# A transformer block on one core: values computed per 64-key block into the attention layout, two chunks with the in-engine softmax division, another order

## The chip, the core and the metric

The kernel runs on one core of a Trainium2 chip. The metric is device microseconds of one execution. The engines of the core work side by side, each through its own list of instructions in order: PE multiplies matrices (its weight loads are listed as PEld), DVE and ACT do element work and empty the accumulators (`ps`, 8 banks), POOL does small element work, SP (and at the start ACT) issues the transfers, which share 16 DMA engines.

## What is computed

One sequence of 2048 tokens, width 448, in bf16. Cut to what matters:

```python
def _A_ref(x, wqkv, wo):                 # x = layernorm(input)
    q, k, v = split(x @ wqkv)            # 16 heads of 28
    # token s looks at the 8 keys s, s-2, ..., s-14 of its own parity (masked below 0)
    attn = softmax(q . k[idx] * 28**-0.5)
    return (attn @ v[idx]) @ wo
def _B_ref(x, w1, w2, w3, w4):           # x = layernorm(h)
    g = gelu(layernorm(x) @ w1)          # 448 wide
    hs = shift4(g) @ w2                  # quarters shifted by -1, +1, -2, +2 tokens
    x1 = x + hs
    return x1 + gelu(layernorm(x1) @ w3) @ w4    # 1792 wide
h   = x + _A_ref(layernorm(x), wqkv, wo)
out = h + _B_ref(layernorm(h), w1, w2, w3, w4)
```

## The kernel before

The tokens are cut into four chunks of 512 (`c` = 0 to 3), each kept as two runs of 256 tokens of even and of odd parity, so that a query sees 8 neighbouring keys of its run. For attention, a run's keys are taken in `NB` = 5 overlapping blocks of 64 (`KS` = 50 apart), the queries in blocks of 51 or 52. Everything is written as operations with declared reads and writes; the list `_ORDER` (line 232) fixes the order on every engine and the bank of each accumulator, and waits follow from the declared reads and writes. The numbers that the helpers take as costs are not used when the kernel runs.

Per chunk these steps run, each line being the code that the prediction's names refer to:

- **A1** (`phase_A1`, 536): layernorm of the tile (BN_STATS, BN_AGGR on DVE; 1/sqrt on POOL; the scaling into `lntm` on DVE or ACT), then the transposition into `hT`. Chunks 0 and 1 (`TPE`) transpose on PE, 16 small matmuls a chunk, and copy to `hT`; chunks 2 and 3 with one DMA transposition of four tiles, issued by SP.
- **V** (`phase_V`, 558): v = hT x wv, 28 matmuls of 64 rows, 128 columns and 448 streamed columns, each pair on the upper and the lower half of the array (`quad`, 368). The result is copied to `vraw`, written by two transfers to a scratch array in DRAM and read back by two more as `vt`, the five 64-key blocks of each parity, key on the partition.
- **QK** (`phase_QK`, 576): q and k, 56 matmuls, into `qk`.
- **S**, **AV** (`phase_att`, 592): 80 small matmuls for the scores of half the heads (`g` = 0, 1), exp on ACT into `pt`, a mask multiplication on DVE, 80 small matmuls with `vt`. One column of `vt` is a constant, so that the sum of each row comes along.
- **Division by that sum**: chunk 0 (`FAST`) with `norm_blocks` (642): for each of its four blocks a 32x32 transposition out of the bank, a reciprocal, a multiplication and a transposition back, all on DVE. Chunks 1 to 3 with `norm_dma` (656): a copy to `osb`, transfers that gather the sums, a reciprocal, a transfer to DRAM, four transfers that spread it, four multiplications on DVE.
- **WO** (`phase_WO`, 680), **B1** (`phase_B1`, 693: residual, two layernorms, W1 and gelu into `gT`), **B2** (W2 and a layernorm), **W3** (`phase_W3`, 750: a transposition by DMA, the adds tagged `R`, W3 and gelu), **B3** (W4, residual, output). B2, W3 and B3 run over five groups of tiles, `g` = 0 to 4, two or four tiles each.

In the program's order S, AV and their neighbours of chunk 0 to 2 stand between the QK and V of later chunks; W1 of chunk 0 comes after S of chunk 2; from WO of chunk 3 on, PE has only W1 to W4 left. SP issues every load of weights, every transposition by DMA and every scratch transfer in one list.

## Time and profile before

| | |
|---|---|
| median of 3 runs | 216.14 us (215.55 to 216.34) |
| the profiled execution | 216.01 us |
| its span, first to last instruction | 214.2 us |
| PE busy | 183.7 us (86%) |
| DVE busy | 120.5 us (56%) |
| ACT, POOL busy | 92.1 us, 52.5 us |
| bytes moved by DMA | 23.53 MB |

The span is the time from the first to the last instruction of the profiled execution; its own time is 1.8 us longer. Busy shares are averages over the whole span. "Issue" as a releaser means that the engine stood idle and waited for nothing that the profile shows. A merged row of the timeline stands for a run of equal matmuls: start, length, and in brackets the idle time ahead of it and what ended it.

### The profile page before, as it was taken

The numbers are of one execution on the slowest core, as the hardware profiler recorded it, in microseconds if no ns is written. First come the engines' busy times: TensorE is split into PE (matmuls) and PEld (weight loads), VectorE is DVE, ScalarE is ACT, GpSimd is POOL, SyncE is SP. The second block draws the span as 40 slices with busy tenths as digits, with TensorE's granted clock in tenths as the row PEclk, the third lists the DMA queues.
The fourth block names the chain that finished last, engine by engine and source line by source line (L and its number), as shares of the span: only waits on it lengthen the run. The fifth ranks groups of instructions, "written<-read, shape, count | busy, mean of one in ns | idle before, by whom it ended". The sixth has DMA issues, their size and how long they took to land.

```text
span 214.2 us, 6051 instructions
## 1 busy us (share of the span) xinstructions
PE 183.7 (86%) x2687; PEld 99.9 (47%) x2687; DVE 120.5 (56%) x250; ACT 92.1 (43%) x111; POOL 52.5 (24%) x108
## 2 busy tenths in 40 slices
...
PEclk9759999999799999999999999999999999999998
DMA  5995949799199924940051870035400091000111
GB/s 149 356 267 138 261 78 252 169 163 268 30 130 200 315 47 81 234 122 0 3 101 54 107 180 18 24 59 123 81 0 0 21 171 43 0 3 6 43 46 49
DMA packets 37568, 23.53 MB, mean 110 GB/s; under 512 B 22800, under 2 KB 36768, under 8 KB 37536
## 3 DMA queue, kind: packets, MB, share of 16 engines
...
## 4 chain that ended last, share of the span: by engine, by line
PE 48%; DVE 18%; DMA 16%; issue 6%; ACT 4%; POOL 4%; SPq 2%; ACTq 0%
PE ps L1236 48%; DMA actT<-lntm 7%; DVE st L1236 5%; DVE xb L1236 5%; DMA rzb<-rz_scratch 4%; DMA arena<-in_A_wqkv_dram 3%; DVE lntm L1236 2%; DVE xin L1236 2%; ACT qk L1236 2%; SPq L1236 2%; DMA rz_scratch<-rzp 2%; POOL rstd L1236 1%; POOL xb L1236 1%; DVE oT L1236 1%; DVE mv L1236 1%
## 5 line engine op out<-in xcount | busy, mean ns | idle before, releaser
L1236 PE MATMUL ps<-actT,w_s 64*128 64x512 bf16 (+3 forms) x672 | 56.1, 323 | 6.7 <-DMA actT<-lntm 3.6
L1236 PEld LDWEIGHTS ps<-actT,w_s 64*128 64x128 bf16 (+1 forms) x672 | 34.5, 99 | 27.8 <-ACT arena L1236 3.3
L1236 PE MATMUL ps<-w_s,arena 128*128 128x448 bf16 x224 | 43.5, 353 | 0.0
L1236 DVE TENSOR_TENSOR xb<-ps,xb 128x448 bf16<-128x448 f32 (+1 forms) x24 | 18.3, 771 | 32.7 <-PE ps L1236 32.7
L1236 ACT ACTIVATE arena<-ps 128x512 bf16<-128x512 f32 (+2 forms) x40 | 28.4, 766 | 17.3 <-PE ps L1236 17.3
L1236 PEld LDWEIGHTS ps<-w_s,arena 128*128 128x128 bf16 x224 | 21.7, 98 | 20.4 <-issue 0.4
L1236 PE MATMUL ps<-hT,arena 64*128 64x512 bf16 x224 | 28.0, 403 | 1.1 <-DVE hT L1236 0.5
L1236 POOL TENSOR_SCALAR vtmp<-mv 128x4 f32<-128x4 f32 (+1 forms) x18 | 4.7, 259 | 91.0 <-DVE mv L1236 90.1
L1236 DVE BATCH_NORM_STATS2 st<-xin 128x6 f32<-128x448 bf16 x32 | 18.4, 608 | 1.1 <-DMA xin<-in_A_x_dram 0.9
L1236 PEld LDWEIGHTS ps<-hT,arena 64*128 64x128 bf16 x224 | 10.9, 100 | 16.0 <-issue 3.4
L1236 ACT ACTIVATE pt<-ps 128x1024 bf16<-128x1024 f32 x16 | 15.5, 1023 | 6.5 <-PE ps L1236 6.5
L1236 ACT ACTIVATE qk<-ps 128x1024 bf16<-128x1024 f32 x10 | 10.1, 1024 | 17.7 <-PE ps L1236 17.7
L1236 POOL TENSOR_TENSOR rstd<-vtmp,mhalf 128x4 f32<-128x4 f32 (+1 forms) x18 | 17.3, 962 | 1.0
L1236 POOL TENSOR_TENSOR xb<-xb,xin 128x448 bf16<-128x448 bf16 x16 | 16.8, 1067 | 2.7 <-ACT lntm L1236 1.9
L1236 PE MATMUL ps<-wo_s,oT 128*128 128x448 bf16 x64 | 13.8, 353 | 3.8 <-issue 2.4
L1236 DVE SCALAR_TENSOR_TENSOR oT<-osb,rzb 128x512 bf16<-128x512 f32 x12 | 7.5, 686 | 14.8 <-DMA rzb<-rz_scratch 14.8
L1236 ACT ACTIVATE lntm<-xb,nmr,rstd 128x512 bf16<-128x512 bf16 x7 | 5.5, 810 | 21.6 <-POOL nmr L1236 21.6
L1236 DVE TENSOR_TENSOR pt<-pt,msk 128x1024 bf16<-128x1024 bf16 x16 | 11.7, 738 | 3.1 <-ACT pt L1236 3.1
L1236 DVE SCALAR_TENSOR_TENSOR xin<-ps,xin 128x896 bf16<-128x896 f32 x8 | 8.6, 1073 | 8.2 <-PE ps L1236 8.2
L1236 PE MATMUL ps<-w_s,gT 112*128 112x448 bf16 x64 | 13.1, 353 | 0.0
L1236 PE MATMUL ps<-arena,hT 64*128 64x448 bf16 x112 | 11.4, 350 | 0.4 <-ACT qk L1236 0.4
L1236 PE MATMUL ps<-pt,vt 64*32 64x51 bf16 (+1 forms) x640 | 6.9, 190 | 5.5 <-issue 4.2
...
## 6 DMA issues: line engine op xcount, KB each, us to landing
rzb<-rz_scratch SPq DMA_DIRECT2D x12, 256.0 KB, 4.3
...
vt<-v_scratch SPq DMA_DIRECT2D x8, 320.0 KB, 5.8
v_scratch<-vraw SPq DMA_DIRECT2D x8, 256.0 KB, 3.7
...
```

The source lines that it names most:

```text
L1236: inst = getattr(eng, meth)(**kw)
```

## The change

**Values.** `hT` gets 8 more columns per parity ahead of a chunk's 256 (copied from the chunk before by POOL), and a layout in which 64 neighbouring keys of one parity are contiguous. V now takes a 64-key block of each parity as its weights and writes the result to the partitions where attention wants it: per chunk 56 matmuls of 64 rows, 64 columns and 448 streamed columns in `quad`, in groups of four that use the four quarters of the array, and 8 of 128 rows and 64 columns for the fifth block (with `wv_2`, a copy of one weight window whose upper half is zero). The banks are copied straight to `vt`, three copies where there were two (896, 896 and 448 elements a partition). `vraw`, the scratch array, its two zero writes, eight writes and eight reads are gone.

**Division.** `FAST` is now chunks 0 and 1: chunk 1 uses `norm_blocks`.

**Moved.** The 16 adds tagged `R` and the zeroing of `wo_s` go from POOL to DVE. The DMA transposition of chunks 2 and 3 is issued tile by tile (eight instead of two). The V weights are loaded ahead of the others.

**Order.** All of `_ORDER` is new. Three places:

PE from its start: the warm-up matmuls (oT), the transpositions of chunk 0 (ident), QK (hT,arena), V (arena,hT; wv_2), the scores S (qk). Before:

```order
L1236 MATMUL ps<-oT 128x512 x14
L1236 MATMUL ps<-ident,lntm 128x128 x16
L1236 MATMUL ps<-hT,arena 128x512 x28
L1236 MATMUL ps<-arena,hT 128x448 x28
L1236 MATMUL ps<-qk 64x52 x8
L1236 MATMUL ps<-qk 64x51 x32
L1236 MATMUL ps<-qk 64x52 x8
L1236 MATMUL ps<-qk 64x51 x32
```

and now:

```order
L1256 MATMUL ps<-oT 128x512 x14
L1256 MATMUL ps<-ident,lntm 128x128 x16
L1256 MATMUL ps<-arena,hT 64x448 x4
L1256 MATMUL ps<-wv_2,hT 64x448 x2
L1256 MATMUL ps<-arena,hT 64x448 x46
L1256 MATMUL ps<-hT,arena 128x512 x28
L1256 MATMUL ps<-arena,hT 64x448 x12
L1256 MATMUL ps<-ident,lntm 128x128 x16
```

V of chunk 0 now stands ahead of the first QK, the last 12 of its matmuls behind it, and 64 matmuls stand where 28 did.

PE ahead of the first W1 (actT,w1_s), where before the second half of QK of chunk 2 (x56), S of chunk 2, V of chunk 3 and S again stand:

```order
L1236 MATMUL ps<-hT,arena 128x512 x56
L1236 MATMUL ps<-qk 64x52 x8
L1236 MATMUL ps<-qk 64x51 x32
L1236 MATMUL ps<-qk 64x52 x8
L1236 MATMUL ps<-qk 64x51 x32
L1236 MATMUL ps<-arena,hT 128x448 x28
L1236 MATMUL ps<-qk 64x52 x8
L1236 MATMUL ps<-qk 64x51 x32
L1236 MATMUL ps<-qk 64x52 x8
L1236 MATMUL ps<-qk 64x51 x32
L1236 MATMUL ps<-actT,w1_s 112x512 x28
```

and now the end of AV of chunk 1 (pt,vt), the first 8 matmuls of V of chunk 3, and the second half of S of chunk 2:

```order
L1256 MATMUL ps<-pt,vt 32x52 x8
L1256 MATMUL ps<-pt,vt 32x51 x32
L1256 MATMUL ps<-pt,vt 32x52 x8
L1256 MATMUL ps<-pt,vt 32x51 x32
L1256 MATMUL ps<-arena,hT 64x448 x4
L1256 MATMUL ps<-wv_2,hT 64x448 x2
L1256 MATMUL ps<-arena,hT 64x448 x2
L1256 MATMUL ps<-qk 64x52 x8
L1256 MATMUL ps<-qk 64x51 x32
L1256 MATMUL ps<-qk 64x52 x8
L1256 MATMUL ps<-qk 64x51 x32
L1256 MATMUL ps<-actT,w1_s 112x512 x28
```

V of chunk 3 is mostly behind W1 now, and AV, V and S of three chunks stand close together.

DVE around the division of chunk 1. Before, it has the reciprocal of the gathered sums (rzp<-zp) and, later, four multiplications (oT<-osb,rzb); in between stand copies, scalings (lntm, xb) and masks (pt):

```order
L1236 CAST qk<-ps 128x4x256
L1236 RECIPROCAL rzp<-zp 128x64
L1236 TENSOR_SCALAR lntm<-xin,mv,rstd 128x512 x3
L1236 CAST qk<-ps 128x4x256
L1236 TENSOR_SCALAR xb<-xin,mv,rstd 128x448 x2
L1236 TENSOR_TENSOR pt<-pt,msk 128x1024
L1236 CAST vraw<-ps 128x32x28
L1236 TENSOR_TENSOR pt<-pt,msk 128x1024 x3
L1236 SCALAR_TENSOR_TENSOR oT<-osb,rzb 128x2x256 x4
L1236 COPY osb<-ps 128x1024
```

and now the division of its first half, with scalings for chunk 0 between its steps:

```order
L1256 STREAM_TRANSPOSE osb<-ps 128x512
L1256 TENSOR_SCALAR lntm<-xin,mv,rstd 128x512 x2
L1256 STREAM_TRANSPOSE osb<-ps 128x512
L1256 TENSOR_SCALAR xb<-xin,mv,rstd 128x448
L1256 RECIPROCAL zp<-osb 128x16
L1256 TENSOR_SCALAR xb<-xin,mv,rstd 128x448
L1256 SCALAR_TENSOR_TENSOR rzb<-osb,zp 128x512
L1256 RECIPROCAL zp<-osb 128x16
L1256 TENSOR_SCALAR xb<-xin,mv,rstd 128x448
L1256 STREAM_TRANSPOSE oT<-rzb 128x2x256
L1256 SCALAR_TENSOR_TENSOR rzb<-osb,zp 128x512
L1256 STREAM_TRANSPOSE oT<-rzb 128x2x256
```

Each block takes a transposition, a reciprocal, a multiplication and a transposition back, and the second half of chunk 1 follows with the same eight instructions.

The diff, cut to its core (of the table the first line stands for all):

```diff
-4 0 18 3 14 17 19 2 1 15 61 20:7 60 76 68 8 12 62 16 69 6 7 63 72 9 70 5 64 11 71 29 93 65 27 13 66 23 28 75 30
+4 0 16 3 56 77 12 15 76 8 1 13 62 17:7 14 61 59 2 9 42 75 60 71 6 7 63 5 69 10 70 73 103 66 26 104 64 24 72 27
...
-    TPE, FAST = (0, 1), (0,)
+    TPE, FAST = (0, 1), (0, 1)
...
-    hT = sb("hT", [128, 2, 4, 4, 128], BF16)
+    hT = sb("hT", [128, 2, 4, 2, 272], BF16)
     qk = sb("qk", [128, 2, 4, 2, 2, 264], BF16)
-    vraw = sb("vraw", [128, 4, 16, 32], BF16)
     vt = sb("vt", [128, 2, NB, 16, 32], BF16)
...
+    wv_2 = sb("wv_2", [128, D], BF16)
...
-    VROW = HALF + 8
-    v_d = nc.dram_tensor("v_scratch", (2 * VROW, 512), BF16, kind="Internal")
...
+        if not isinstance(outs[0], list):
+            outs = [[o] for o in outs]
+            lhsTs = [lambda r, w, f=f: [f(r, w)] for f in lhsTs]
         lo, hi = slice(0, 64), slice(64, 128)
 
         def phase(a, b, ba, bb, first, T):
             mms = []
             for x, y in zip(ba, bb):
-                mms.append((outs[a], lhsTs[a](lo, x), rhss[a](lo, x), first and x == ba[0], not first and x == ba[-1]))
-                mms.append((outs[b], lhsTs[b](hi, y), rhss[b](hi, y), first and y == bb[0], not first and y == bb[-1]))
-            op = pe(mms, len(mms) * (n / 4.8 + 1.5), "half")
+                for k, r, v, bv in ((a, lo, x, ba), (b, hi, y, bb)):
+                    for o, l in zip(outs[k], lhsTs[k](r, v)):
+                        mms.append((o, l, rhss[k](r, v), first and v == bv[0], not first and v == bv[-1]))
+            op = pe(mms, 2 * len(ba) * (n / 4.8 + 1.5), "half")
...
+    win_load("wqk", wqk_s, A_wqkv[:, 0:2 * D], 512 * 2 * D * 2, ("sp", "act"))
     win_load("wv", wv_s, A_wqkv[:, 2 * D:3 * D], 512 * D * 2, ("sp", "act"))
-    win_load("wqk", wqk_s, A_wqkv[:, 0:2 * D], 512 * 2 * D * 2, ("sp", "act"))
...
-    tag("vz")
-    for p in range(2):
-        dma("vz%d" % p, v_d.ap()[p * VROW:p * VROW + 8, :], zz[0:8, :], 8192)
...
-    pool("memset", 312, ap=vraw[:, :, :, 29:32], constant=0.0)
-    pool("memset", 141, ap=vraw[:, :, :, 28], constant=2.0 ** -4)
+    pool("memset", 100, ap=hT[:, 0, :, :, 8:16], constant=0.0)
...
+        for s in range(2):
+            pool("memset", 330, ap=vt[:, s, :, :, 29:32], constant=0.0)
+            pool("memset", 200, ap=vt[:, s, :, :, 28], constant=2.0 ** -4)
...
-        pool("memset", 1589, ap=wo_s[:], constant=0.0)
+        dve("memset", 600, ap=wo_s[:], constant=0.0)
...
-    def transpose_pe(ls, il, dst):
+    def columns(s, il):
+
+        o = 16 + 128 * (il % 2)
+        return hT[:, s, :, il // 2, o:o + 128]
+
+    def transpose_pe(ls, il, s):
...
-        copy(dst[:, il, :, :], T(bv), 512, mode=2.0)
-
-    def transpose_dma(ls, dst, n):
-
-        S.add_many("sp", [("dma_start_transpose", dict(
-            out=dst[:, 0:n, :, :].rearrange("p i w n -> p (i w) n"),
-            in_=lntm[:, ls, 0:n, :, :].rearrange("p i a k -> p (i a k)")))], 600 + 310 * n, 600 + 310 * n,
-            chan="tr%d" % ls, nbytes=n * 131072, fix=600)
+        copy(columns(s, il), T(bv), 512, mode=2.0)
+
+    def transpose_dma(name, dst, src, n):
+
+        S.add_many("sp", [("dma_start_transpose", dict(out=dst, in_=src))], 600 + 310 * n, 600 + 310 * n,
+            chan="tr%s" % name, nbytes=n * 131072, bw=194.0, fix=400)
+
+    def transpose_tiles(ls, dst, n):
+        transpose_dma("%d" % ls, dst[:, 0:n, :, :].rearrange("p i w n -> p (i w) n"),
+                      lntm[:, ls, 0:n, :, :].rearrange("p i a k -> p (i a k)"), n)
...
         for il in range(4):
             normalize(0, 0, 4 * c + il, lntm[:, ls, il, :, :], windows(xin[:, 4 * c + il, :]), dve_only=c == 0)
             if c in TPE:
-                transpose_pe(ls, il, hT[:, s, :, :, :])
-        if c not in TPE:
-            transpose_dma(ls, hT[:, s, :, :, :], 4)
+                transpose_pe(ls, il, s)
+            else:
+                transpose_dma("%d_%d" % (c, il), columns(s, il), lntm[:, ls, il, :, :].rearrange("p a k -> p (a k)"), 1)
+        if c > 0:
+            tag("Vc_%d" % c)
+            pool("tensor_copy", 215, out=hT[:, s, :, :, 8:16], in_=hT[:, 1 - s, :, :, 264:272])
...
     def pad_wqk():
+        tag("padv")
+        dve("memset", 230, ap=wv_2[:], constant=0.0)
+        copy(wv_2[64:128, :], wv_s[64:128, 2, :], D, psum=False, mode=3.0)
...
     def phase_V(c):
+
         s = c % 2
         tag("V_%d" % c)
-        T1, T2 = tile(2), tile(2)
-        quad([T(lambda p, u=u: p[:, u, 0:D]) for T in (T1, T2) for u in range(2)],
-             [lambda r, w, k=k: hT[r, s, k, w, :] for k in range(4)],
+        T1, T2, T3 = tile(2), tile(2), tile()
+        halves = lambda T, u: [T(lambda x, u=u, p=p: x[64 * p:64 * p + 64, u, 0:D]) for p in range(2)]
+        keys = lambda r, w, b: [hT[r, s, w, p, 8 + KS * b:72 + KS * b] for p in range(2)]
+        quad([halves(T, u) for T in (T1, T2) for u in range(2)], [lambda r, w, b=b: keys(r, w, b) for b in range(4)],
              [lambda r, w: wv_s[r, w, :]] * 4, D, T1, T2)
+        tag("V_%d.4" % c)
+        pe([(o, l, wv_2[:] if w == 2 else wv_s[:, w, :], w == 0, w == 3) for w in range(4)
+            for o, l in zip(halves(T3, 0), keys(slice(0, 128), w, 4))], 4 * (D / 2.4 + 2.5), "full")
+        v = lambda p: p[:, :, 0:D].rearrange("p u (j d) -> p u j d", d=28)
         for k, T in enumerate((T1, T2)):
             tag("V_%d.e%d" % (c, k))
-            copy(vraw[:, 2 * k:2 * k + 2, :, 0:28],
-                 T(lambda p: p[:, :, 0:D].rearrange("p u (j d) -> p u j d", d=28)), 2 * D)
-        tag("Vd_%d" % c)
-        for p in range(2):
-            dma("vw%d" % p, bass.AP(v_d, (p * VROW + 8 + 256 * c) * 512, [[512, 128], [128 * 512, 2], [1, 512]]),
-                vraw[:, 2 * p:2 * p + 2, :, :].rearrange("k u j d -> k u (j d)"), 128 * 2 * 1024)
-            dma("vr%d%d" % (s, p), vt[64 * p:64 * p + 64, s, :, :, :].rearrange("k b j d -> k b (j d)"),
-                bass.AP(v_d, (p * VROW + 256 * c) * 512, [[512, 64], [KS * 512, NB], [1, 512]]), 64 * NB * 1024)
+            copy(vt[:, s, 2 * k:2 * k + 2, :, 0:28], T(v), 2 * D)
+        tag("V_%d.e2" % c)
+        copy(vt[:, s, 4:5, :, 0:28], T3(v), D)
...
-                 [lambda r, w: hT[r, s, :, w, :]] * 4, 512, T1, T2)
+                 [lambda r, w: hT[r, s, w, :, 16:272]] * 4, 512, T1, T2)
...
-        transpose_dma(ls, actT[:, a, :, :, :], 4)
+        transpose_tiles(ls, actT[:, a, :, :, :], 4)
...
         for c, il in grp:
             i = 4 * c + il
-            pool("tensor_tensor", 1040, out=xb[:, i, :], in0=xb[:, i, :], in1=xin[:, i, :], op=ALU.add)
+            dve("tensor_tensor", 390, out=xb[:, i, :], in0=xb[:, i, :], in1=xin[:, i, :], op=ALU.add)
```

## Rows read from the trace of the kernel before

**Rows 1.** The page's part 1: busy us, share of the span, instructions.

```profile
PE 183.7 (86%) x2687; PEld 99.9 (47%) x2687; DVE 120.5 (56%) x250; ACT 92.1 (43%) x111; POOL 52.5 (24%) x108
```

**Rows 2.** The page's part 2, 40 slices: granted clock and DMA share in tenths.

```profile
PEclk9759999999799999999999999999999999999998
DMA  5995949799199924940051870035400091000111
```

**Rows 3.** Timeline of PE: start, length, run [idle before <-releaser]; first transpositions, QK, V.

```profile
10.73 2.10 PE L1236 MATMUL ps<-ident,lntm 128*128 128x128 bf16 x16 [4.56 <-DVE lntm L1236]
13.35 4.00 PE L1236 MATMUL ps<-hT,arena 64*128 64x512 bf16 x28 [0.52 <-DVE hT L1236]
17.19 2.81 PE L1236 MATMUL ps<-arena,hT 64*128 64x448 bf16 x28
```

**Rows 4.** Timeline of DVE at the start: the copy of the padded weights, the first scalings.

```profile
8.29 0.40 DVE L1236 COPY arena<-arena 128x896 bf16<-128x896 bf16 x1 [1.69 <-DMA arena<-in_A_wqkv_dram]
8.60 2.72 DVE L1236 TENSOR_SCALAR lntm<-xin,mv,rstd 128x512 bf16<-128x512 bf16 x4
```

**Rows 5.** Timeline of PE: the stops inside runs of matmuls; QK at two speeds.

```profile
35.86 0.55 PE L1236 MATMUL ps<-qk 28*64 28x51 bf16 x47 [0.80 <-issue]
...
39.59 0.23 PE L1236 MATMUL ps<-pt,vt 64*32 64x51 bf16 x11 [1.13 <-issue]
...
47.27 1.88 PE L1236 MATMUL ps<-wo_s,oT 128*128 128x448 bf16 x9 [2.35 <-issue]
...
52.02 0.49 PE L1236 MATMUL ps<-pt,vt 64*32 64x51 bf16 x42 [1.63 <-issue]
52.44 7.90 PE L1236 MATMUL ps<-hT,arena 64*128 64x512 bf16 x56
...
73.26 0.94 PE L1236 MATMUL ps<-pt,vt 64*32 64x51 bf16 x93 [1.45 <-issue]
...
78.78 3.19 PE L1236 MATMUL ps<-hT,arena 64*128 64x512 bf16 x28
```

**Rows 6.** Timeline of PE: 80 matmuls of AV, and the run behind them.

```profile
112.34 0.80 PE L1236 MATMUL ps<-pt,vt 64*32 64x52 bf16 x80 [0.87 <-DVE pt L1236]
113.08 4.72 PE L1236 MATMUL ps<-actT,w_s 64*128 64x256 bf16 x56
```

**Rows 7.** Timeline of PE: the waits ahead of W1, W3 and WO.

```profile
67.83 3.23 PE L1236 MATMUL ps<-actT,w_s 64*112 64x512 bf16 x28 [2.44 <-ACT pt L1236]
...
87.00 5.61 PE L1236 MATMUL ps<-actT,w_s 64*128 64x128 bf16 x112 [1.65 <-DMA actT<-lntm]
...
133.39 0.93 PE L1236 MATMUL ps<-wo_s,oT 128*128 128x448 bf16 x4 [1.32 <-DVE xb L1236]
```

**Rows 8.** Groups by shape, DVE: the division, block by block and behind the transfers.

```profile
L1236 DVE SCALAR_TENSOR_TENSOR oT<-osb,rzb 128x512 bf16<-128x512 f32 x12 | 7.5, 686 | 14.8 <-DMA rzb<-rz_scratch 14.8
...
L1236 DVE STREAM_TRANSPOSE osb<-ps 128x512 f32<-128x512 f32 x4 | 2.6, 693 | 0.9 <-PE ps L1236 0.9
...
L1236 DVE SCALAR_TENSOR_TENSOR rzb<-osb,zp 128x512 bf16<-128x512 f32 x4 | 2.5, 670 | 0.0
...
L1236 DVE RECIPROCAL zp<-osb 128x16 f32<-128x16 f32 x4 | 0.7, 222 | 0.0
```

**Rows 9.** Groups by shape: the adds on POOL, a bf16 operation on DVE, copies of qk.

```profile
L1236 POOL TENSOR_TENSOR xb<-xb,xin 128x448 bf16<-128x448 bf16 x16 | 16.8, 1067 | 2.7 <-ACT lntm L1236 1.9 <-DVE lntm L1236 0.8
...
L1236 DVE TENSOR_TENSOR pt<-pt,msk 128x1024 bf16<-128x1024 bf16 x16 | 11.7, 738 | 3.1 <-ACT pt L1236 3.1
...
L1236 DVE CAST qk<-ps 128x1024 bf16<-128x1024 f32 x6 | 7.3, 1224 | 5.8 <-PE ps L1236 5.8
```

**Rows 10.** The page's part 6: scratch transfers, KB each, us to landing.

```profile
vt<-v_scratch SPq DMA_DIRECT2D x8, 320.0 KB, 5.8
v_scratch<-vraw SPq DMA_DIRECT2D x8, 256.0 KB, 3.7
```

**Rows 11.** Busy time by stage: length, PE, PEld, DVE, ACT, POOL, granted clock, DMA share, GB/s.

```profile
10.73:68.00 57.27, 47.08 (x1130) 24.88 (x1132) 43.80 (x92) 31.37 (x37) 9.17 (x23) 0.93 0.81 177
68.00:134.00 66.00, 58.26 (x954) 32.95 (x952) 40.26 (x76) 34.10 (x41) 16.56 (x30) 1.00 0.50 107
134.00:208.20 74.20, 73.47 (x593) 40.35 (x591) 28.79 (x64) 23.59 (x31) 17.91 (x30) 1.00 0.21 45
```

**Rows 12.** Timeline of PE: its last run.

```profile
192.10 16.06 PE L1236 MATMUL ps<-w_s,arena 128*128 128x448 bf16 x84
```

More of the change, by code (lines that the diff above doesn't have):

```diff
@@ new lines @@
+299 501 435 300 434 605:6 502 444:24 606a 436 508 303 445 614 506 509 446 507 514 516 447 515 438:60 517 523
+518v 448 439 524 520v 521v 440 519v 449 525 522 526 441 527v 442 529v 450:42 530v 528v 443 612:6 451 613v 452
+615 453 454 531:60 455 532 533 616 534 617 535 456:24 457 536 458 619 459 460 618 537:0 621 461 620 538 544:4
+539 545 540 471:7 546 541 549 542 547 462:6 543 548 550 472 551 553 622 552 624 554 625 557a 626:4 555v 558a 562
+627 560 556a 563 468:7 623 559 561 463 628 464 629:0 634 632 630 635 633 469 465:6 631 470 638 636 473 639 637
@@ L357, in pool, with name_x @@
         return S.add_many("pool", [(meth, kw)], lat - 20, lat)
+    def name_x(chan):
+        return chan[0] == "x"
     def dma(chan, out_ap, in_ap, nbytes, eng="sp", issue=430.0, bw=290.0):
```

55 lines of the change are left out of this document (25 added, 30 removed), and 7 rows, old and new, of the table _ORDER.

## The prediction

> **What bounds the kernel now.** I read the busy shares first, then PE's list in order of time, then the busy time by stage. PE is busy 183.7 us [rows 1], and its last matmul ends at 192.10 + 16.06 = 208.2 us [rows 12]. The profiled execution took 216.0 us: 1.8 lie around the span, 6.0 behind that last matmul (the last residual, its transfer, the closing check), and before it PE stands idle for 208.2 - 183.7 = 24.5 us. The change touches neither end, so the question is how much of the 24.5 goes, and what PE gets to do in addition.
>
> By stage [rows 11]: up to 68 us PE is busy 47.1 of 57.3 us, so 10.2 idle; up to 134 us 58.3 of 66.0, so 7.7 idle; from then on 73.5 of 74.2, and nothing is left to win but work. Ahead of the first transpositions it waits 4.6 us [rows 3].
>
> The reader should look at what the idle pieces are. The largest class is five stops in the middle of a run of equal matmuls, with no releaser: 0.80, 1.13, 2.35, 1.63 and 1.45 us, 7.4 together [rows 5]. Counted through PE's order they come at matmul 475, 603, 729, 856 and 1237, that is 126 to 128 matmuls apart or three times that, and every matmul has a weight load: a stop after each 256 instructions, which is PE waiting for its own instructions. The next block comes 3.7, 7.7 and 4.8 us after the one before it (35.86 to 39.59 to 47.27 to 52.02). The 80 matmuls of S or AV use up their 160 instructions in 0.74 us [rows 6], so a block that holds two such runs is gone sooner than the next has come; and DMA is at nine tenths in most slices of that time [rows 2]. The granted clock falls to 0.7 in one slice [rows 2], a mean of its two levels, 2.4 and 1.2 GHz, right after PE has stopped for 2.35 and 1.63 us: 56 matmuls of QK take 7.90 us where 28 take 3.19 later [rows 5], so 1.5 us lost. The second class is waits for results: W1 of chunk 0 2.44, W3 1.65, WO of chunk 3 1.32 us [rows 7]. No wait of PE is released by the read of `vt`: the trip through DRAM is long (3.7 and 5.8 us [rows 10]) but hidden by an order that puts AV late. Taking it out is worth only what a better order makes of it, and the bytes: 8 x (320 + 256) KB, 4.6 of 23.53 MB.
>
> **V on PE.** Before, 28 matmuls a chunk in 14 pairs take 2.81 us, 201 ns a pair [rows 3]. Now there are 14 groups of four and 4 pairs for the fifth block. If the four quarters of the array run together, a chunk costs 18 x 201 ns = 3.62 us, 0.81 more, 3.2 for four chunks. If only the two halves of the rows run together, as before, it is (28 + 8) x 201 ns = 7.2 us, 4.4 more, 17.7 for four. A gain is excluded, since more columns are streamed than before. The nearest row is AV [rows 6]: tiles of 64 rows and 32 columns, 80 in 0.74 us (112.34 to 113.08), 9.25 ns each. By the V row 51 columns take 201 x 51/448 = 23 ns, so 2.5 run at once, although the rows offer only two places. Tiles on the same rows and different columns do overlap. I take 3.2. The third copy out of the banks, four times half a `qk` copy of 1.22 us [rows 9], so 2.4, lies on DVE and ACT beside PE.
>
> **The start.** The first scaling on DVE stands behind a copy that waits 1.69 us for the QK weights [rows 4]; PE's transpositions wait for the scalings, QK for them [rows 3]. In the new order the scalings stand ahead of the copies and V, whose weights come first, ahead of QK. The most that this gives is 2.6 us (QK at 13.35 moved to the place of the transpositions at 10.73), the least 0, if the statistics of chunk 1, which now stand between the scalings, wait for their own input. I take **1.5 us off**, near the wait that goes.
>
> **Up to the first W1** (67.83 before). The work is what it was but for V: three chunks grew (2.4), the first 0.8 of chunk 3 is here, its other matmuls (2.81 before) are behind W1: +0.4. The slow QK was a result of the stops; -1.5. Of the 10.2 idle, 5.9 are stops. The new order thins S and AV out with V and QK, and by the same count of 127 all blocks but two hold 3.4 us of work or more. The two are those from matmul 984 and 1111 (66 of S, 12 of V, 49 of AV: 0.6 + 0.6 + 0.45 = 1.7 us; then 31, 8 of V, 80 and 8 of W1: 0.3 + 0.4 + 0.75 + 0.9 = 2.35). With a refill of 3.7 us they stop PE for 2.0 and 1.35; with the others 3.5. The ends are 0, if less traffic makes the refill short, and 12, with 7.7 us for each. The rest of the idle time, 4.3, I put at 3.5. The stage becomes 47.1 + 0.4 - 1.5 + 7.0 = 53.0, **4.3 off**. DVE must fit: it is busy 43.8 us here. `norm_blocks` for chunk 1 costs 4 x (2 x 0.693 + 0.222 + 0.670) = 9.1 us against 4 x 0.686 = 2.7 [rows 8], half of that difference here, +3.2; three `qk` copies fewer are -3.7. 43.3 of 53 us fits, with little room ahead of a WO.
>
> **From the first W1 to WO of chunk 3** (134). Work is pulled in: 14 groups of V of chunk 3 (2.8), 14 matmuls of W4 (16.06/84 each [rows 12], 2.7) and 8 of W2 (1.5): 58.3 becomes 65.3. Idle stays about the same for other reasons. WO of chunk 1 now waits for DVE, not for transfers: after the second AV of that chunk two blocks of 2.28 us must be done, between masks: I put 2.5, with 0 to 6 for the ends. WO of chunk 3 still goes through the transfers. Before, it came 20.3 us after its last AV began to drain (113.1 to 133.4); the new order has W3, W1, W2 and W4 for some 16 us between them, but no transposition between the reciprocal and its transfer on SP; 2.5. The rest 2.3. Together 7.3 against 7.7. The stage becomes 72.6, **6.6 more**. The 16 adds that leave POOL (1.07 each [rows 9]) cost DVE between 0.32 (a mask's 738 ns scaled to 448 elements) and 1.07 each; at the lower, nearer end 5 us spread over 130, hidden while DVE is busy 40 of 66 us; if it were not, they would sit ahead of output tiles that PE does not wait for soon. The eight tile-wise transpositions on SP stand behind weight loads; V of chunk 2 waits for them, some 10 us after their inputs. I put nothing for that.
>
> **From WO of chunk 3 on.** PE is full; the 4.2 us of W4 and W2 done earlier are gone from here: **4.2 off**.
>
> Sum: -1.5 - 4.3 + 6.6 - 4.2 = -3.4, so **212.6 us** against 216.0 of the profiled execution (the median of the runs, 216.1, is 0.1 above; no difference that matters). The 3.2 of V are within these terms.
>
> **Rivals.**
> *The stops go and the waits with them.* With a fifth of the bytes gone the refill keeps up (stops 3.5 to 0.5), the two waits for WO are half (-2), the start gives all 2.6 (-1.1): 206.5 us. For it: the order is thinned out, DMA was at nine tenths. Against: no stretch of the trace shows a refill under 3.7 us. Chance 0.24.
> *The columns do not overlap.* V costs 7.2 us a chunk: 14.5 above my term; some 4 of it would fill waits of the first two stages: 223 us. This ends slower from the point where a chunk's V costs over 4.5 us (3.4 / 4 above 3.62). Against it stands the 9.25 ns of AV; for it, that no row shows 64 x 64 tiles streaming 448 columns. Chance 0.12. The Trainium skill, page "TensorE: Matmul & The Clock Gate", Part 3, says that a weight load overlaps running matmuls only when its row group differs; a quarter's load would then wait for its neighbour on the same rows. The AV rows speak against it as a general rule here.
> *The refill gets slower.* More instructions (144 matmuls more, each with a load) and eight transpositions where two were: at 7.7 us a block the stops are 9.5 instead of 3.5, 2 of it under waits that are there anyway: 216.6 us, no difference. Chance 0.12.
> *DVE becomes the bound.* The blocks of two chunks, masks, statistics and adds stand in one list; if WO of chunk 1 waits 8 us for it instead of 2.5, the time is 218 us. It decides from a wait of 6. For: 43 of 53 us busy; against: half of chunk 1's division is after W1. Chance 0.10.
>
> **The numbers.** My forecast has the remaining 0.42. The first rival and nearly all of the forecast are faster, the third is the same with the upper edge of the forecast, the second and the fourth are slower. About 0.5%, 1.1 us, is what a measurement of this kernel can tell from no change. Faster 0.64, same 0.14, slower 0.22. The range from 205.5 to 218.5 takes in all but the columns that do not overlap and the far ends of the stops.
>
> **What would show it.** V of a later chunk: 3.5 to 3.9 us for 64 matmuls (right), over 5 (columns serial). Stops without releaser inside S and AV: two, near matmul 1111 and 1238, 3.5 us in all. First V before 12 us. QK at 3.2 us per 28 everywhere but the first. First W1 near 62 us, WO of chunk 3 near 134, from there on nearly no idle time. DVE as the releaser of WO of chunk 1. The forecast is wrong if W1 comes after 66 us, or if a new wait over 4 us stands behind 62 us.

## The result, and the profile after

The changed kernel takes **203.9 us** (median of 4 runs, 203.0 to 204.6) against 216.2 us of the kernel before (215.6 to 217.5): a ratio of **0.942**, interval 0.936 to 0.948. The forecast was 212.6 with a range from 205.5: the sign was right, the gain was 12 us instead of 3.4, and the time lies below the range. (Where some executions of a version were disturbed, the medians below are those of the others.)

The profiled execution took 204.0 us, its span is 202.3. From its page: part 1, the granted clock and the DMA share by slices, the packets, and the transfers of PE's own instructions (before: [rows 1, 2]):

```profile
PE 188.9 (93%) x2831; PEld 102.5 (51%) x2831; DVE 121.1 (60%) x275; ACT 96.8 (48%) x118; POOL 37.3 (18%) x97
...
PEclk9969999999995999999999999999999999999997
DMA  6997055667620005920260554062400262000111
...
DMA packets 32265, 17.69 MB, mean 87 GB/s; under 512 B 22376, under 2 KB 31720, under 8 KB 32232
...
q8 instruction: 24, 0.39, 0.8%
```

PE does 5.2 us more work and is still done sooner. The three stages of the prediction (up to the first W1; to WO of chunk 3; to PE's end), each kernel cut at its own marks: length, PE busy, PEld, DVE, ACT, POOL, granted clock, DMA share, GB/s. First the kernel before:

```profile
0.00:67.83 67.83, 51.84 (x1142) 26.45 (x1143) 50.62 (x111) 34.27 (x40) 17.99 (x48) 0.92 0.81 188
67.83:133.39 65.56, 57.81 (x950) 32.79 (x951) 39.82 (x76) 34.27 (x41) 16.56 (x30) 1.00 0.51 109
133.39:208.16 74.77, 74.07 (x595) 40.68 (x595) 29.40 (x64) 23.59 (x31) 17.91 (x30) 1.00 0.21 44
```

and the changed kernel:

```profile
0.00:59.85 59.85, 51.70 (x1230) 26.07 (x1231) 47.45 (x116) 36.08 (x43) 19.53 (x53) 0.97 0.64 161
59.85:127.73 67.88, 67.53 (x1030) 37.78 (x1030) 45.76 (x97) 35.83 (x42) 11.05 (x27) 0.95 0.33 66
127.73:197.43 69.70, 69.70 (x574) 38.60 (x572) 27.26 (x64) 24.87 (x33) 6.75 (x18) 1.00 0.21 49
```

Length minus PE busy is idle time: 16.0, 7.7 and 0.7 us before, 8.2, 0.35 and 0 now. In all PE idles 8.5 us ahead of its last end instead of 24.5 (-16.0); it is busy 5.2 longer; the part of the span behind it is 4.9 instead of 6.0 (-1.1). That makes the 12. The last of these belongs to no step: over the versions below it lies anywhere from 4.2 to 6.

The waits of PE that are left in the changed kernel (waited for; us in total, times, longest):

```profile
PE ps L1256 <- DVE lntm L1256: 4.0, 2, 2.8
PE ps L1256 <- issue: 2.3, 2, 2.0
PE ps L1256 <- DVE oT L1256: 1.2, 1, 1.2
PE ps L1256 <- DVE hT L1256: 0.4, 1, 0.4
PE ps L1256 <- DVE qk L1256: 0.3, 1, 0.3
```

None of the waits of [rows 7] is among them. What is left is the start and the stops without a releaser. (The two repeats of the changed kernel, below, have a further wait of 0.8 us for a transposition by DMA.) PE's timeline at the start, then around the long stop:

```profile
7.53 0.40 PE L1256 MATMUL ps<-ident,lntm 128*128 128x128 bf16 x4 [1.19 <-DVE lntm L1256]
10.71 0.84 PE L1256 MATMUL ps<-ident,lntm 128*128 128x128 bf16 x12 [2.78 <-DVE lntm L1256]
11.96 0.96 PE L1256 MATMUL ps<-arena,hT 128*64 128x448 bf16 x4 [0.40 <-DVE hT L1256]
...
55.34 0.53 PE L1256 MATMUL ps<-pt,vt 64*32 64x52 bf16 x47
57.82 0.40 PE L1256 MATMUL ps<-pt,vt 64*32 64x52 bf16 x33 [1.95 <-issue]
...
59.85 1.50 PE L1256 MATMUL ps<-actT,w_s 64*112 64x512 bf16 x5
61.68 5.19 PE L1256 MATMUL ps<-actT,w_s 64*112 64x512 bf16 x23 [0.34 <-issue]
66.80 0.81 PE L1256 MATMUL ps<-pt,vt 64*32 64x52 bf16 x80
67.54 2.63 PE L1256 MATMUL ps<-wo_s,oT 128*128 128x448 bf16 x13
```

One stop of 1.95 us sits inside the second AV of chunk 1, one of 0.34 inside W1 of chunk 0; that W1 then runs at 226 ns a matmul, where 28 of them take 3.23 us elsewhere (115 ns): the lower of the clock's two levels, some 3 us lost. The clock is down before the short stop: it was granted at 0.50 in the five matmuls ahead of it and at 0.52 behind it. WO of chunk 1, at 67.54, waits for nothing.

### The profile page after: what moved, and what is told of

Read it like the earlier page. It is cut to its first block, busy times and chain, and to the rows that moved or that the text cites. A ratio compares the mean times of both kernels' runs of the same rounds, so it can differ in the third digit from the quotient of the medians.

```text
span 202.3 us, 6332 instructions
## 1 busy us (share of the span) xinstructions
PE 188.9 (93%) x2831; PEld 102.5 (51%) x2831; DVE 121.1 (60%) x275; ACT 96.8 (48%) x118; POOL 37.3 (18%) x97
## 4 chain that ended last, share of the span: by engine, by line
PE 87%; DMA 4%; DVE 3%; issue 2%; POOL 1%; ACT 0%; SPq 0%; POOLq 0%
PE ps L1256 87%; DMA xin<-in_A_x_dram 4%; DVE st L1256 1%; DVE lntm L1256 1%; DVE qk L1256 1%; POOL rstd L1256 1%; ACT vt L1256 0%; POOL vt L1256 0%; SPq L1256 0%; DVE xb L1256 0%; POOL nmr L1256 0%; DVE hT L1256 0%; POOL vtmp L1256 0%; DVE mv L1256 0%; POOL hT L1256 0%
## 5 line engine op out<-in xcount | busy, mean ns | idle before, releaser
L1256 PE MATMUL ps<-actT,w_s 64*128 64x256 bf16 (+3 forms) x672 | 59.6, 333 | 0.3 <-issue 0.3
L1256 PEld LDWEIGHTS ps<-actT,w_s 64*128 64x128 bf16 (+1 forms) x672 | 35.8, 103 | 23.3 <-issue 4.8
L1256 DVE TENSOR_TENSOR xb<-ps,xb 128x448 bf16<-128x448 f32 (+1 forms) x24 | 18.4, 767 | 40.8 <-PE ps L1256 40.8
L1256 PE MATMUL ps<-hT,arena 64*128 64x512 bf16 x224 | 25.9, 377 | 0.5 <-DVE qk L1256 0.3
L1256 POOL TENSOR_TENSOR rstd<-vtmp,mhalf 128x4 f32<-128x4 f32 (+1 forms) x18 | 18.2, 1011 | 0.9
L1256 PE MATMUL ps<-arena,hT 64*64 64x448 bf16 (+1 forms) x248 | 17.2, 375 | 0.4 <-DVE hT L1256 0.4
L1256 ACT ACTIVATE qk<-ps 128x1024 bf16<-128x1024 f32 x13 | 12.9, 1021 | 6.5 <-PE ps L1256 6.5
L1256 DVE TENSOR_SCALAR lntm<-xin,mv,rstd 128x512 bf16<-128x512 bf16 x23 | 8.2, 401 | 5.6 <-POOL nmr L1256 5.2
L1256 ACT ACTIVATE lntm<-xin,nmr,rstd 128x512 bf16<-128x512 bf16 x9 | 7.0, 806 | 9.4 <-POOL nmr L1256 9.4
L1256 PEld LDWEIGHTS ps<-arena,hT 64*64 64x64 bf16 (+1 forms) x248 | 7.3, 113 | 7.9 <-issue 2.4
L1256 DVE TENSOR_TENSOR pt<-pt,msk 128x1024 bf16<-128x1024 bf16 x16 | 10.4, 673 | 1.4 <-ACT pt L1256 1.4
```

The source lines that it names most:

```text
L1256: inst = getattr(eng, meth)(**kw)
```

## The experiments

Each version runs beside the kernel before on the same chip; the ratio is to that, in brackets its 95% interval. "Idle" is PE's idle time ahead of its last end, "stops" the part without a releaser, both from the version's profile; three numbers or two are repeats, and "(one)" or "(two)" is the number of executions behind a time, where they are so few.

| version | us | ratio | idle | stops |
|---|---|---|---|---|
| before | 216.2 | 1 | 24.5 | 7.7 |
| after | 203.9; 202.9; 203.3 | 0.942; 0.935; 0.946 | 8.5; 9.5; 10.0 | 2.3; 2.5; 2.6 |
| E1 new parts, old order | 212.4; 212.8 | 0.976 [0.965, 0.986]; 0.975 [0.968, 0.981] | 18.4; 19.2 | 1.7; 2.0 |
| E2 V through DRAM, rest new | 206.1 (two) | | 15.0 | 6.0 |
| E3 chunk 1 divided by transfers | 213.6 | 0.983 [0.972, 0.994] | 17.2 | 3.1 |
| E4 adds on POOL | 204.1 | 0.939 [0.929, 0.949] | 9.5 | 2.6 |
| E5 old parts, new order | 222.2 | 1.016 [1.009, 1.023] | 27.8 | 7.2 |
| E6 before, no trip of V | 213.5 | 0.991 [0.984, 0.997] | 22.2 | 3.1 |
| E7 after, 4.2 MB more | 206.6 | 0.958 [0.944, 0.972] | 11.7 | 4.9 |
| E8 after, 80 instructions more | 205.9 (one) | | 11.2 | 4.9 |
| E9 short matmuls spread | 199.3 (one; all 4: 202.6) | | 8.8 | 0.6 |
| E10 start in another order | 203.1 | 0.938 [0.929, 0.948] | 7.0 | 2.6 |
| E11 E9 and E10 | 200.5; 200.2 | 0.927 [0.917, 0.937]; 0.934 [0.926, 0.941] | 9.7; 6.3 | 0.9; 0.3 |
| E12 E11, other banks | 202.0 | 0.936 [0.919, 0.953] | 10.6 | 2.0 |
| E13 3 us delay on DVE | 202.2 | 0.942 [0.917, 0.967] | 9.8 | 3.3 |
| E14 6 us delay on DVE | 206.9 | 0.965 [0.953, 0.977] | | |

### Order or parts: the four corners

**E1**: the operations of the changed kernel in the order of the kernel before. Operations were matched by step; the new ones were placed so:

```diff
-VRAW, Vd, vz; copies, sums and broadcasts of chunk 1's division
+V_c.4 (fifth block) behind the first copy of V of chunk c, chunk 1: behind QK of chunk 1
+N_1.g: transpositions where O_1.g was, reciprocals where Z_1 was, the rest where N_1 was
+Vc_c behind the transpositions of chunk c; R adds in the same place, on DVE
```

> All new parts (V by 64-key block into the attention layout, chunk 1 divided by transpositions on VectorE, one-tile transpositions of chunks 2 and 3, weights of QK first, the residual adds on VectorE) stand in the old queue order; the fifth block of V and the extra halo copies are put right behind the V they belong to. Theory A, the order is what hides the waits: the stops of PE and the named waits of the kernel before stay (over 18 us idle before the last matmul instead of 24.5, since only the wait of WO of chunk 1 can go), PE has 3 us more work, so 213 to 219 us. Theory B, the parts themselves (fewer bytes, a shorter division) shorten the stops and waits whatever the order: under 14 us idle, 205 to 209 us.

Measured: 212.4 us, 18.4 idle, stops 1.7. Half of each theory: the time and the idle time are nearly those of theory A, the stops those of theory B. The named waits stayed without the new order; most of the stops went without it, though E1 also moves PE's instructions against the 256th ones that the stops fall on (below). PE's waits in E1, the larger ones:

```profile
PE ps L1254 <- DVE lntm L1254: 4.1, 2, 3.4
PE ps L1254 <- DMA actT<-lntm: 3.3, 3, 1.5
PE ps L1254 <- ACT qk L1254: 2.3, 2, 1.5
PE ps L1254 <- DVE oT L1254: 2.1, 2, 1.2
PE ps L1254 <- issue: 1.7, 1, 1.7
```

Once more, on the chip of E5:

> The new parts in the old order once more, beside the new order with the old parts on one chip: 0.97 to 0.985 of the kernel before, 211 to 213.5 us.

212.8 us, 0.975 [0.968, 0.981]; the same.

**E2**: one part undone in the new order.

```diff
-keys = lambda r, w, b: [hT[r, s, w, p, 8 + KS * b:72 + KS * b] for p in range(2)]
+quad(..., [lambda r, w, k=k: columns(s, k)[r, w, :] for k in range(4)], ...)   # 128-token tiles
+dma("vw%d" % p, <v_scratch>, vraw[...]); dma("vr%d%d" % (s, p), vt[...], <v_scratch>)
```

> The changed kernel in its own order, but V is computed by 128-token tiles and goes through the DRAM scratch as before: PE loses 3.2 us of V, the transfers get 4.6 MB back, and AV of a chunk waits for write and read (3.7 and 5.8 us). Theory A: V of chunk 2 is copied by 56.6, so vt is there at about 66, just when AV of chunk 2 comes at 66.7; nothing new waits for long, and the time is 201 to 204.5 us. Theory B, the bytes made the stops: the refills are slow again, the stops of PE grow from 2.3 to 5 us or more, and the time is 205 to 209 us.

206.1 us, some 2 above E4, which ran on the same chip and equals the changed kernel. PE works 2.6 us less, but idles 6.5 more (5.0 against the third profile of the changed kernel): 6.0 of its 15.0 are stops, 1.0 is a wait of AV of chunk 2 for `vt`. Two of the stops, in PE's timeline:

```profile
31.54 0.70 PE L1251 MATMUL ps<-pt,vt 64*32 64x51 bf16 x67 [0.76 <-issue]
...
37.30 0.36 PE L1251 MATMUL ps<-pt,vt 64*32 64x51 bf16 x26 [3.75 <-issue]
```

So in this profile the trip through DRAM, which no wait of the trace before named, costs more in stops than V straight into its layout costs in work. The time is less sure: its two executions, 205.0 and 207.2, overlap the 202.7 to 205.1 of E4. And E2 changes the number of PE's instructions together with the bytes; only E6 and E7 change the bytes alone.

**E3**: the other part undone.

```diff
-TPE, FAST = (0, 1), (0, 1)
+TPE, FAST = (0, 1), (0,)
```

> The changed kernel in its own order, but chunk 1 is divided as before, with the sums sent through DRAM and broadcast. In the changed kernel the second AV of chunk 1 ends at 59.8 and WO of chunk 1 starts at 67.5 without a wait; chunk 3, which still goes through transfers, needs 10 us and more from its AV to the end of its multiplications. Theory C, the new order needs the short division: WO of chunk 1 waits 2.5 to 6 us and the time is 206 to 210 us. Theory A in its plain form, order alone: the wait is hidden, and DVE with 6 us less work gives 203 to 204.5 us.

213.6 us, 9.4 above E4. WO of chunk 1, in PE's timeline, and behind it DVE's multiplications, which wait for the broadcast:

```profile
74.38 4.67 PE L1254 MATMUL ps<-wo_s,oT 128*128 128x448 bf16 x16 [7.75 <-DVE oT L1254]
```

```profile
62.41 0.55 DVE L1254 RECIPROCAL rzp<-zp 128x64 f32<-128x64 f32 x1 [5.87 <-DMA zp<-osb]
...
72.43 2.50 DVE L1254 SCALAR_TENSOR_TENSOR oT<-osb,rzb 128x512 bf16<-128x512 f32 x4 [7.73 <-DMA rzb<-rz_scratch]
```

Theory C, and more than its 206 to 210: from reciprocal to multiplication 10 us, and WO waits 7.75 of them.

**E4**: `dve("tensor_tensor", 390, ...)` of the R adds back to `pool(...)`.

> The changed kernel with the 16 residual adds back on GpSimd (1.07 us each instead of 0.39 on VectorE), nothing else. Theory A: no wait of PE is released by them, 203.3 to 204.6 us. Rival: GpSimd's inverse deviations, which stand in its queue behind the adds, come late and the transpositions of the next group with them: 205.5 us or more.

204.1 us: no difference that can be told, as theory A has it.

**E5**: E2, E3 and E4 in one. The tile-wise transpositions and the layout of `hT` stay new, so the parts are not quite the old ones.

> The new order with the old parts: V through the DRAM scratch, chunk 1 divided by transfers, the residual adds on GpSimd (the one-tile transpositions, the order of the loads, and the layout of hT stay new). If the costs of undoing V (3 to 4 us) and the division (9.6) add, it takes 215 to 219 us, as long as the kernel before, and the order alone is worth nothing: it is built on the parts. Theory A in its plain form, order alone hides the waits: under 209 us.

222.2 us against 218.0 of the kernel before on that chip, above the 215 to 219 that were expected: **the new order alone loses**. Its waits of PE, the largest:

```profile
PE ps L1251 <- DVE oT L1251: 9.2, 2, 8.0
PE ps L1251 <- issue: 7.2, 3, 4.4
PE ps L1251 <- DVE lntm L1251: 4.8, 2, 2.8
```

The four corners as ratios: old parts and old order 1; new parts alone 0.975; new order alone 1.016; both 0.942. The two do not add: 0.975 x 1.016 would be 0.991. The order gains only with the parts, and the parts gain less than half of it without the order. The new order puts WO of chunk 1 some 9 us behind its last AV; the division on DVE is done in 6 of them, the transfers need 15.6 (E3: 59.3 to 74.9). And the parts, left in the old order, meet the old waits.

### What makes the stops

Counted in instructions through PE's list (two for a matmul, one for a wait of its own), the stops of the kernel before come at instruction 958, 1214, 1471, 1727, 2239 (0.29 us, at 65.07) and 2495, those of the changed kernel at 2239 and 2495: 256, or a multiple, apart, but for one instruction. Three versions ask what makes them long.

**E6**: the kernel before without V's round trip. V is copied straight into `vt`, where its rows do not belong, and the fifth block is a constant, so AV's result is another one; PE's work is the same.

```diff
-copy(vraw[:, 2 * k:2 * k + 2, :, 0:28], ...)
+copy(vt[:, s, 2 * k:2 * k + 2, :, 0:28], ...)
-dma("vw%d" ...); dma("vr%d%d" ...)
```

> The kernel before, in its own order, without the round trip of V: V's four tiles are copied straight into the place that AV reads, so AV gets the wrong values of V (the fifth block is a constant), and the 4.6 MB of writes and reads through the scratch are gone. PE's work is that of the kernel before. Theory B, the bytes make the stops: the stops of PE fall from 7.4 to 2 us or so as with the new parts in the old order (1.7), QK of chunk 2 is not slowed, and the time is 207 to 211 us. Theory A, the order of the short matmuls alone makes them: the stops stay at 6 us or more, 213 to 216 us.

213.5 us against 215.2 on that chip; stops 3.1 instead of 7.7:

```profile
42.10 0.27 PE L1224 MATMUL ps<-pt,vt 64*32 64x51 bf16 x10 [2.50 <-issue]
...
71.95 0.93 PE L1224 MATMUL ps<-pt,vt 64*32 64x51 bf16 x92 [0.57 <-issue]
```

The time is 1.7 us shorter, just clear of none. The constants' memsets on POOL put the first transpositions 1.0 us later (11.73 instead of 10.73); if that 1.0 is added, the bytes are worth 2.7. The named waits stayed (for ACT's `pt` 2.6 us, for the transposed `actT` 3.8). The stops are nearer to theory B, the time, 213.5, lies in theory A's 213 to 216 and not in theory B's 207 to 211: shorter stops did not make the kernel shorter by as much.

**E7**: the changed kernel with transfers that nobody waits for.

```diff
+dma("jw%d" % p, <scratch, 256 KB in rows of 1 KB>, w4_s[:, 8:11, :] ...)
+dma("jr%d" % p, junk[64 * p:64 * p + 64, :, :], <256 KB of B_w4>)     # p = 0, 1, four chunks
```

> The changed kernel with 4.2 MB of transfers that nobody waits for, of the size and rows of V's old round trip, at the places where V is copied: four writes and four reads of 256 KB per two chunks. Nothing else is changed. Theory B: the stops of PE grow from 2.3 to 4 us or more, above all where they fall beside these transfers, and the time by 2 to 5 us. If the bytes do nothing, within 0.7 us of the changed kernel.

206.6 us (204.3 to 206.9), stops 4.9; the changed kernel has 201.5 to 204.6 on other chips, and stops of 2.3 to 3.3 in the six profiles with PE's order unchanged and no bytes added (its own three, E4, E10, E13). In PE's timeline the stops of the changed kernel and one more, which stands 256 instructions times three ahead of the next (the 27th matmul of S):

```profile
42.16 0.61 PE L1264 MATMUL ps<-qk 28*64 28x51 bf16 x54 [0.80 <-issue]
...
57.66 0.40 PE L1264 MATMUL ps<-pt,vt 64*32 64x52 bf16 x33 [2.15 <-issue]
...
63.17 5.36 PE L1264 MATMUL ps<-actT,w_s 64*112 64x512 bf16 x23 [1.93 <-issue]
```

The last block comes 5.5 us after the one ahead of it; in the changed kernel 3.9 (57.82 to 61.68), in E13 4.1. So the bytes alone make the refill slower.

**E8**: `+ [(T(lambda p: p[:, 0, 0:8]), zz[:, 0:128], zz[:, 0:8], True, True)] * 40` behind the warm-up.

> The changed kernel with 40 tiny matmuls (8 columns) more behind the warm-up, 80 instructions, in a time in which PE waits anyway. If PE's stops belong to the 256-instruction blocks, the long stop moves 40 matmuls ahead in the program: from the 47th to the 7th of the 80 of the second AV of chunk 1, shorter since the block ahead of it then holds 2.85 us of work instead of 1.7 (0.5 to 1 us); the next comes in the middle of the second S of chunk 2 (its 46th) instead of in W1 of chunk 0, longer (1 to 2 us), since its block holds 2.0 instead of 2.5. If the stops belong to the operations, they stay where they are.

```profile
35.91 0.20 PE L1257 MATMUL ps<-pt,vt 64*32 64x51 bf16 x3 [1.54 <-issue]
...
57.94 0.54 PE L1257 MATMUL ps<-qk 28*64 28x52 bf16 x46
61.84 0.45 PE L1257 MATMUL ps<-qk 28*64 28x52 bf16 x34 [3.36 <-issue]
```

The second stop is where it was expected, behind the 46th matmul of S, and PE's list has instruction 2495 there again; the first is at 1215, not at the place I had named, which passes without a stop. So the places follow the count, and the sizes do not follow from what one block holds: 3.36 us behind a block of 2.0 us of work, a refill of 5.5 us (56.32 to 61.84) with no traffic added. The Trainium skill, page "Runtime: NRT & Kernel Launch", section "Instruction fetch mechanics", says that instructions are fetched in blocks of 256 and that the cost of crossing one is mostly hidden. The rows agree on the 256, and not on the second where blocks of short matmuls stand beside full queues.

The packed traces settle more of it, for they hold the transfers of PE's instructions, 16 KB each: the 24 of `q8 instruction` on the page above. At each of the 42 stops of over 0.25 us without a releaser, in all profiles together, PE goes on 1.2 to 1.5 us after such a transfer has ended, and the transfer itself takes 0.9 to 2.3. What differs most is when it begins, counted from the first matmul of the block ahead, from 0.6 to 6.5 us. With the queues nearly empty it begins after 1.3 us (changed kernel, from 57.82; DMA share 0.01) and 1.9 (E13, from 57.30; 0.04). Beside other transfers it begins after 2.9 in E7 (from 57.66; 0.89), and after 5.0 and 5.8 in the kernel before (from 39.59 and 65.07, queues full). So E8's long stop is traffic too, the kernel's own: its block ahead starts at 56.32, a load of 448 KB keeps the queues busy until 59.4, and the transfer of the instructions begins at 59.38. In the changed kernel the same load is through at 57.3, before its block starts. What stays open is why one such transfer waits 1.6 us (kernel before, from 35.86) and another 5.8, both beside full queues.

### Versions that spread them

**E9** moves S of chunk 2 and AV of chunk 1 among longer matmuls, E10 puts the scalings of chunk 0 ahead of the statistics of chunk 1 (and lets PE transpose the tiles as they get ready). In `_ORDER` (operation:bank):

```diff
 # E9, PE only: V_2 is 332 to 335, S_2.0 474, AV_1.1 323, V_3.4 357, S_2.1 481, W1_0 252 to 255
-332 333 334 474 335 323 357 481 252 253 254 255
+332 333 474 334 335 357 323 252 253 481 254 255
 # E10, DVE only: scalings 36 33 30, copies 35 32, pads 45 44, statistics of chunk 1 111 107 108 109 110 105
-36 111 107 33 108 30 109 35 110 32 105 55 45 44
+36 33 30 35 32 45 44 111 107 108 109 110 105 55
```

E9:

> The changed kernel with three operations of PE moved, to spread the short matmuls over the instruction blocks around the long stop: S of chunk 2's first half up by 12 matmuls of V, the second AV of chunk 1 behind the fifth block of V of chunk 3, S of the second half into the middle of W1 of chunk 0 (and the bank numbers behind it exchanged). The block that held 1.7 us of work now holds 3.0, the next 2.9 instead of 2.5. Theory A, a block that is used up sooner than the next one comes makes the stop: the stop falls from 1.95 us to under 1.0, W1 of chunk 0 runs faster, and the time falls by 1 to 4 us against the changed kernel. Rival: the stop belongs to the transfers of that time, not to what the block holds: it stays near 2 us and the time within 0.7 us.

E10:

> The changed kernel with the start of VectorE's list in another order: the scalings of chunk 0 and the copies of its transposed tiles stand ahead of the statistics of chunk 1, and the four transpositions come in the order in which their tiles are ready. In the changed kernel PE waits 2.78 us for those scalings while VectorE waits 1.32 us for the transfer of chunk 1. If that wait is the one that ends last, V of chunk 0 starts at about 10.3 us instead of 11.96 and the time falls by 1 to 1.7 us; if the weights or the transposed tiles end last anyway, it stays within 0.5 us.

E11, both:

> Both of the edits above in one. If they act in different places, the gains add: 2 to 5.5 us below the changed kernel, 198.5 to 202 us. If the start only moves the wait to the next transfer or stop, the time is that of the better of the two.

> The version with both edits (short matmuls spread, start in another order) once more, with more runs: 1.5 to 4 us below the changed kernel if the stop and the wait at the start are worth what their traces showed (2.2 us of stop and 1.7 us at half clock, 1.2 us of the start, less 2.1 us of new waits).

E9 alone cannot be told from the changed kernel with the runs that it has, though its profile has lost the long stop: one of 0.6 us is left. Nor can E10 (203.1 against 202.9): V starts at 10.31 as was hoped, and the 1 to 1.7 us did not show in the time. Both together can: 200.5 beside 202.9 of the changed kernel on one chip, and, with more runs, 200.2 us (199.9 to 201.1) beside 203.3 (201.5 to 203.7) on another, **3.2 us less**. Its timeline (second profile), first the start of V, then the place of the long stop:

```profile
10.10 0.95 PE L1254 MATMUL ps<-arena,hT 128*64 128x448 bf16 x4
...
55.10 0.57 PE L1254 MATMUL ps<-arena,hT 128*64 128x448 bf16 x4 [1.37 <-ACT pt L1254]
...
59.72 0.25 PE L1254 MATMUL ps<-qk 28*64 28x51 bf16 x11 [0.26 <-issue]
59.89 1.50 PE L1254 MATMUL ps<-actT,w_s 64*112 64x512 bf16 x12
62.13 0.80 PE L1254 MATMUL ps<-pt,vt 64*32 64x52 bf16 x80 [0.73 <-ACT pt L1254]
```

V starts at 10.10 instead of 11.96; the stop of 1.95 is gone, the one behind it is 0.26 at the same instruction (2495); W1 runs at full clock. In return there are two new waits for the exponentials, 2.1 us.

**E12** tries to take the first of these away with other banks (V_3.4 to 4, AV_1.1 to 5 and 3, W1_0 to 6 and 0).

> The version with both edits (spread matmuls, start), and other PSUM banks for four tiles: the fifth block of V of chunk 3 takes a bank that a copy of V of chunk 2 has freed, instead of one that the exponentials of chunk 2 still read. In the version before it waits 1.37 us for those. Expected: that wait goes or halves, 0.5 to 1.2 us less than with both edits; if another wait takes its place, the same.

The wait fell to 0.45 us, but the profile has stops of 0.60, 0.70 and 0.70: 202.0, no gain that can be told. One more of its executions took 1032 us; the cause is open, and the version is not one to take.

The changed kernel as the measure of these, twice:

> The changed kernel as it is, on the chip of the next three, as their measure: 203 to 205.5 us. Its one long stop of PE should come at the same matmul (the 47th of the 80 of the second AV of chunk 1).

> The changed kernel as it is, the measure for the others of this call: 202.5 to 205 us.

203.5 and 203.4 over all runs; the stop came at the 47th matmul each time (2.19 and 2.30 us).

### How much room stands ahead of WO of chunk 1

DVE's list after the second AV of chunk 1 in the changed kernel: from the first transposition to the last, with the masks between, 58.32 to 64.08, while PE has V, S, W1, AV and half of WO to do:

```profile
58.32 1.31 DVE L1256 STREAM_TRANSPOSE osb<-ps 128x512 f32<-128x512 f32 x2 [1.73 <-PE ps L1256]
...
63.38 0.70 DVE L1256 STREAM_TRANSPOSE oT<-rzb 128x512 bf16<-128x512 bf16 x1
```

E13 and E14 put memsets ahead of that last transposition:

```diff
+for k in range(2):        # E14: 4
+    dve("memset", 1500, ap=junk[:], constant=0.5)      # 128 x 1536, 1.73 us from one to the next
```

> The changed kernel with two memsets of 1.44 us, 2.9 in all, on VectorE ahead of the last transposition of chunk 1's division. In the changed kernel that transposition ends at 64.1 and WO of chunk 1 starts at 67.5. If those 3.5 us are true slack (the second stage's idle time, put at 7.3 in the prediction, is gone because the division was ready long before it was asked for), WO of chunk 1 waits for under 0.5 us and the time stays within 0.7 us of the changed kernel. If DVE is nearly the bound there, each us shows: 2 us or more.

> The same with four memsets, 5.8 us. By the slack of 3.5 us WO of chunk 1 now waits 2 to 2.6 us for VectorE and the time rises by 1.5 to 3 us; with no slack by 5 to 6, with DVE free behind it by under 1.

E13: 202.2 us, no more than the changed kernel. In its PE timeline:

```profile
64.91 1.69 PE L1258 MATMUL ps<-wo_s,oT 128*128 128x448 bf16 x8
66.99 1.68 PE L1258 MATMUL ps<-wo_s,oT 128*128 128x448 bf16 x8 [0.40 <-ACT gT L1258]
```

and on DVE the delayed transposition:

```profile
66.19 0.65 DVE L1258 STREAM_TRANSPOSE oT<-rzb 128x512 bf16<-128x512 bf16 x1
```

3.5 us of delay are swallowed but for 0.4. The wait is put down to ACT's `gT`, which ends at 67.01; but in the changed kernel the second half of WO runs from some 69.1 on while the same `gT` lasts until 69.64, so that it is DVE's transposition, done at 66.84, that the wait is for. E14, 6.9 us of delay: 206.9, 3.5 us more. Its profiled execution took 278.8 us at a mean granted clock of 0.65, for a cause that is open; in it the second half of WO waits 2.2 us for DVE. Both versions agree on a slack of 3 us or a little more: the division is not nearly the bound, and not free without end. In the changed kernel's own profile, where W1 ran at the lower clock and WO came later, the rows leave some 5 us (64.08 to 69.1); in E13 W1 ran at the higher one.

## Why the prediction was wrong, step by step

- **The step that failed: "idle stays about the same for other reasons".** The second stage was given 7.3 us of idle time (2.5 for WO of chunk 1, 2.5 for WO of chunk 3, 2.3 for the rest); it has 0.35. For WO of chunk 1 only DVE's side was worked out, for WO of chunk 3 the transfers were taken to need nearly as long as before, and the rest had no row. They could have been worked out: DVE needs 5.8 us (58.32 to 64.08) for WO of chunk 1, and PE has 7.3 us of matmuls meanwhile (V 0.9, S 0.8, W1 3.2, AV 0.75, and 1.65 of the first half of WO, which reads the other half of `oT`), besides its stops; E13 and E14 find some 3 us of slack. Against chunk 3's transfers the new order has 15.3 us of work on PE (112.42, the end of its last AV, to 127.73), and the transfers no longer need so long: the multiplications start 17.2 us after the last AV before (from 113.1), behind a wait of 12 us, and 13.9 after it now, behind none:

```profile
130.30 2.50 DVE L1236 SCALAR_TENSOR_TENSOR oT<-osb,rzb 128x512 bf16<-128x512 f32 x4 [11.99 <-DMA rzb<-rz_scratch]
...
126.28 1.89 DVE L1256 SCALAR_TENSOR_TENSOR oT<-osb,rzb 128x512 bf16<-128x512 f32 x3
```

- **What this step makes, and the rest.** Idle in the second stage -7.0 from the forecast, in the first -3.1 (8.2 instead of 11.3), in the last -0.7, behind PE -1.1, and PE busy 3.5 more than foreseen (188.9 instead of 185.4, most of it W1 at the lower clock): -8.4, the 8.6 between 212.6 and 204.0 but for rounding.
- **The stops: place right, size too large.** Forecast near matmul 1111 and 1238, 3.5 us; found at 1109 and 1235, 2.3 us. The places, counted ahead, held; the size needs the traffic as well as what a block holds (E6, E7, E8). The prediction's sum for 7.7 us a block does not come out either way: 7.7 less 1.7 and 2.35 of work makes 11.4 for two stops, where it has 12 as the end of the range and 9.5 in the third rival.
- **V on PE: right.** 56 of V's matmuls, 14 groups of four, take 2.84 us in the changed kernel, as long as 14 pairs before (2.81), and the fifth block some 0.9: 3.7 a chunk, against 3.62. Four quarters of the array do run at once; the rival of columns that do not overlap is out.

```profile
76.05 2.84 PE L1256 MATMUL ps<-arena,hT 64*64 64x448 bf16 x56
```

- **The trip of V "is worth only what a better order makes of it, and the bytes": right, and the bytes were too small.** I gave them nothing in the sum. In the new order the profile with them has 3.7 us more of stops (E2, which moves the instructions as well); in the old one the time without them is 1.7 us shorter (E6).
- **The start: right.** 1.5 us off was the forecast; V comes at 11.96 where QK came at 13.35, 1.4 off. The reason why not more was named: chunk 1's statistics wait for their input. In E10 and E11, where they stand behind, V starts 1.65 and 1.86 us sooner still.
- **First W1 near 62, WO of chunk 3 near 134:** 59.85 and 127.73. **DVE as the releaser of WO of chunk 1:** no wait at all. **R adds hidden:** yes (E4). **One-tile transpositions cost nothing:** no wait of PE names them.
- **The rivals.** The nearest was the first, stops and waits gone together, 206.5; it had stops of 0.5 where 2.3 are left, and it too kept half of the waits. Slower refills: not here, but in E8. DVE as the bound: decided from a wait of 6 us; with the slack of E13 and E14 that would take some 9 us of delay, which no run tried.
- **The order was treated as one more part.** E1 and E5 show that parts without the order are worth -2.5%, the order without the parts +1.6%, and both -5.8%.
